# When the weights of the first MLP are narrowed, and when the right operands of the second token group are made

## The chip, the cores and the metric

The kernel runs on one core of a Trainium2 chip. The metric is the device time of one execution in microseconds (us). The engines are TensorE (PE; its weight loads are listed apart as PEld), VectorE (DVE), ScalarE (ACT) and GpSimd (POOL); SyncE (SP) issues almost all transfers.

## The reference, cut to what matters

```
kv  = einsum(k, v)                 # per batch and head, 64 x 64
out = einsum(q, kv);  out = out / rms(out) * g_norm
x   = out as [2304 tokens, 512]
x   = relu(x @ w_in)**2 @ w_out    # first MLP: 512 -> 2048 -> 512; its weights arrive as float64
for e in 0..3:                     # second MLP: 4 experts, 512 -> 1024 -> 512 each
    h    = relu(x @ w1[e])
    out += p[:, e] * (h @ w2[e])   # p: domain_probs, normalised
```

## The kernel before

**Precision.** Each float32 operand of a matmul is kept as two fp32r parts, a head (`hi`, made by ACT as a copy) and a remainder (`lo` = full - `hi`, made by a subtraction). A product is three matmuls for each slab of 128: `lo`·`hi`, `hi`·`lo`, `hi`·`hi`. `split` (L145) makes both parts: ACT, then POOL.

**Tiling.** The tokens form five blocks: 0 to 3 of 512 tokens, 4 of 256. The hidden width is cut into slices of 256. Slices 0 to 7 are the first MLP; slices 8 to 23 are the second MLP for the first token group (blocks 0, 1 and 4), slices 24 to 39 the same weights for the second group (blocks 2 and 3), loaded and prepared again (`slice_of`).

**Units.** The program is a list of small units, written out: `RAMP` (L49) for attention together with slices 0 and 1, `rest()` (L88) for all that follows. `run` (L542) calls one function per unit:

- `k`, `o`, `c`, `b`: attention and its normalisation.
- `f v.j.c` (`g1`): first product of slice v for block j, half c: 12 matmuls, then for the first MLP relu `r`, square `s`, head `hh` on ACT and remainder `hl` on POOL.
- `g v.j.c` (`g2a`): second product of the first MLP: 6 matmuls, then DVE adds to `acc` (L397).
- `s v.b.i` (`g1s`): the pair of blocks b and b+1 takes seven products in place of eight (`PRODUCTS`): the left operands are sums of weight tiles, the right operands are quarters of the pair's activations (`b11`, `b12`, `b21`, `b22`) and sums of them (`t1` to `t4`). 6 matmuls each, into the banks `pa` to `pd`; ACT copies the first result (`p1`), DVE forms `u2` (L480), `u4` (L482) and three more sums, each followed by relu (`hh`, L499) and remainder (`hl`, L500). `pc` and `pa`, `pd` are added to once more by later products, after `u4` and `p1` have been read.
- `h v.j.t` (`g2b`): second product of the second MLP: 6 matmuls, then DVE scales by p and adds (L522). The last slice of a group stores the rows.
- `x g.i` (`right`, L410): makes one tile of right operands for group g: two names of `OPS` at a time, for two slabs k each; `x0.4` makes the operand `xb` of block 4. The tiles `o` have the four buffers of the tag `xs`, which the first MLP's activations, and then group 1's operands, hold before. `t_sum` (L431) makes a sum anew for each name, with the sums that it is made of: 14 subtractions a group (L437). A sum's head is made by ACT (L428), its remainder by DVE (L429).
- `w` (`split_w`, L190): the next unit of weights, in a fixed order: four quarters for each of the slices 0 to 7, two halves for each later slice. Each begins the load of the unit two further on (`load_w(i + 2)`, SP queue, two raw buffers). A quarter of the first MLP is narrowed from float64 (`narrow`): six DVE steps (L171 to L185), a head on ACT (L221), two POOL steps (L222, L223). Half `.0` of a later slice (`operands`) is four sums on DVE (L238 to L241) and four splits into the left operands `a` and `a2`; half `.2` is two splits into `b`. The left operands have three buffers (`a2` two).

**What sets the order.** The units' place in the list is their priority. At build time a planner gives each engine its queue: it draws a ready instruction ahead where an engine would be idle, and gives out the buffers of a tag (the eight of `tmp` hold `r`, `s`, `u`, `k`, `p1`, `u2`, `u4`, the weight sums and the `t` sums) as the list asks for them. On the chip each engine runs its queue in order and waits where an input is late.

Each of the slices 2 to 7 is five blocks: `f` of a block, then `g` of the block before it, and here and there one `w`. A slice of group 1 is seven `s` with `h` of block 4 of the slice before among them, then `f` and `h` of the blocks. A slice of group 2 is seven `s`, each followed by an `h` of the slice before.

Of the kernel before, what the change touches and what calls it, by code (L numbers as in the profile page):

```python
# [10 lines left out]
F32 = mybir.dt.float32  # L11
# [4 lines left out]
ALU = mybir.AluOpType  # L16
PSUM = bass.MemoryType.PSUM

P = 128
# [11 lines left out]
NS1 = DFF // FS  # L31
NS2 = E * F2 // FS
# [20 lines left out]
b13 g0.1.1 c7 f0.2.1 g0.1.2 b15 b14 g0.1.3 w p g0.2.0 b17 g0.2.1 f0.3.0 f0.3.1 g0.2.2  # L53
g0.2.3 b16 w g0.3.0 g0.3.1 f1.0.0 g0.3.2 w f1.0.1 g0.3.3 f0.4.0 f0.4.1 g1.0.0 g1.0.1
g0.4.0 w g0.4.1 w g0.4.2 g1.0.2 w g0.4.3 g1.0.3 f1.1.0 f1.1.1 f1.2.0 f1.2.1 w w g1.1.0
g1.1.1 g1.1.2 g1.2.0 w w g1.2.1 g1.1.3 f1.3.0 g1.2.2 g1.2.3 w w f1.3.1 f1.4.0 g1.3.0
g1.3.1 g1.3.2 g1.3.3 w f1.4.1
""".split()


# [2 lines left out]
GRP2 = (((0, 1), (4,)), ((2, 3),))  # L63
# [7 lines left out]
def second(v, blk):  # L71
    if v < NS1:
        return [f"g{v}.{j}.{c}" for j in blk for c in range(KD)]
    return [f"h{v}.{j}.{t}" for j in blk[::-1] for t in range(BLK[j][1] // P)]


def merge(first, others):

    r, n = [], 0
    for i, u in enumerate(first):  # L80
        r.append(u)
        want = (i + 1) * len(others) // len(first)
        r += others[n:want]
        n = want
    return r


def rest():  # L88
    r, prev = [], (1, (NB - 1,))
    for v in range(2, NS1):  # L90
        for j in range(NB):
            r += [f"f{v}.{j}.{fc}" for fc in range(FC)] + second(*prev)
            if j < (4, 4, 4, 2, 2, 1)[v - 2]:
                r += ["w"]
            prev = (v, (j,))
            if v == NS1 - 1 and j >= 2:
                r += [f"x0.{j - 2}"]
    for g, group in enumerate(GRP2):
        for v in range(NS1 + g * NS2, NS1 + (g + 1) * NS2):
            for blk in group:  # L100
                b = blk[0]
                if v == NS1 and b == 0:
                    r += second(*prev) + ["x0.3"]
                    prev = (v, ())
                if v == NS1 and b == 4:
                    r += ["x0.4"]
                if v == NS1 + NS2:
                    r += [f"x1.{i}" for i in range(4)]
                if len(blk) == 2:
                    units = [f"s{v}.{b}.{i}" for i in range(7)]  # L110
                else:
                    units = [f"f{v}.{b}.{fc}" for fc in range(FC)]
                r += ["w"] * (blk == group[0]) + merge(units, second(*prev)) + ["w"] * (blk == group[-1])
                prev = (v, blk)
    return r + second(*prev)


@with_exitstack
def fused_kernel(ctx, tc, kvm, kvt, qt, g2, probs, w64, w32, out):
    nc = tc.nc  # L120
# [7 lines left out]
    tmp = ctx.enter_context(tc.tile_pool(name="tmp", bufs=8))  # L128
# [16 lines left out]
    def split(hi, lo, full):  # L145
        nc.scalar.activation(out=hi, in_=full, func=AF.Copy)  # L146
        nc.gpsimd.tensor_tensor(out=lo, in0=full, in1=hi.bitcast(F32), op=ALU.subtract)  # L147
# [60 lines left out]
    def split_first(i, v, c):  # L208
        if c == 0:
            w_t[v] = [  # L210
                wp.tile([P, 2, k, n], F32R, tag=t, name=f"{t}{v}")
                for t, k, n in (("a", KD, FS), ("b", FC, DM))
            ]
        w = w_t[v][c // 2]
        n = w.shape[2] // 2
        part = slice(c % 2 * n, c % 2 * n + n)
        r = raw.pop(i)
        hi, lo = (w[:, a, part, :].rearrange("p k f -> p (k f)") for a in range(2))
        if r.dtype == I64:
            top, rest = narrow(r, f"{v}_{c}")  # L220
            nc.scalar.activation(out=hi, in_=top, func=AF.Copy)  # L221
            nc.gpsimd.tensor_tensor(out=top, in0=top, in1=hi.bitcast(F32), op=ALU.subtract)  # L222
            nc.gpsimd.tensor_tensor(out=lo, in0=top, in1=rest, op=ALU.add)  # L223
        else:
            split(hi, lo, r)
# [178 lines left out]
    o_t, t_tmp = {}, {}  # L404

    def x_part(pair, name, k):

        return acc_t[pair[int(name[2]) - 1]][:, (int(name[1]) - 1) * 2 + k, :]

    def right(g, i):  # L410

        pair, *alone = GRP2[g]
        if i == 4:
            (j,) = alone[0]
            x_t[j] = xp.tile([P, 2, KD, BLK[j][1]], F32R, tag="xt", name=f"xb{j}", bufs=1)
            for k in range(0, KD, 2):
                split(*(x_t[j][:, a, k : k + 2, :] for a in range(2)), acc_t[j][:, k : k + 2, :])
            return
        o = xp.tile([P, 2, 4, 512], F32R, tag="xs", name=f"o{g}_{i}", bufs=4)
        for m, name in enumerate(OPS[i]):  # L420
            o_t[pair[0], name] = (o, m * 2)
            for k in range(2):
                hi, lo = o[:, 0, m * 2 + k, :], o[:, 1, m * 2 + k, :]
                if name[0] == "b":
                    split(hi, lo, x_part(pair, name, k))
                    continue
                full = t_sum(pair, name, k)
                nc.scalar.activation(out=hi, in_=full, func=AF.Copy)  # L428
                nc.vector.tensor_tensor(out=lo, in0=full, in1=hi.bitcast(F32), op=ALU.subtract)  # L429

    def t_sum(pair, name, k):  # L431

        b11, b12, b21, b22 = (x_part(pair, f"b{x}", k) for x in ("11", "12", "21", "22"))

        def sub(m, a, b):
            t = tmp.tile([P, 512], F32, tag="tmp", name=f"{m}_{name}_{pair[0]}_{k}")
            nc.vector.tensor_tensor(out=t, in0=a, in1=b, op=ALU.subtract)  # L437
            return t

        if name == "t3":  # L440
            return sub("t3", b22, b12)
        t1 = sub("t1", b12, b11)
        if name == "t1":
            return t1
        t2 = sub("t2", b22, t1)
        return t2 if name == "t2" else sub("t4", b21, t2)


    PRODUCTS = (
# [76 lines left out]
    def probs_p():  # L526
# [9 lines left out]

    unit = dict(
        k=att_kv, o=att_a, c=att_c, b=att_b, w=split_w, p=probs_p, f=g1, g=g2a, x=right, s=g1s, h=g2b
    )
    ext = None  # L540
# [32 lines left out]
    for name in rest():  # L573
        run(name)
# [47 lines left out]
```

## Time and profile before

| | |
|---|---|
| median of three timed runs | 1236.81 us (1235.37 to 1237.0) |
| the profiled execution | 1238.97 us, of which the profile's span 1237.2 us |
| PE, PEld busy | 1206.5 us (98%), 1012.0 us (82%) |
| DVE, ACT, POOL busy | 797.5 (64%), 427.3 (35%), 486.0 us (39%) |
| mean granted clock of PE | 0.991 of 2.4 GHz |

PE is busy almost throughout, and a busy PE can still be a slow one: its clock is granted at one of two levels, 1.2 or 2.4 GHz, and a matmul's busy time grows when it is low. So the time lost in a stretch is found by comparing its length with what its matmuls take at the rate of an undisturbed stretch. "<- DVE u L482" behind a wait names the instruction that ended it.

### The profile page before, as it was taken

How to read it: one execution, taken by the hardware profiler on the slowest of the kernel's cores; microseconds unless marked ns; L12 is line 12 of the kernel's file. 1: busy time of each engine (PE TensorE's matmuls, PEld its weight loads, DVE VectorE, ACT ScalarE, POOL GpSimd, SP SyncE). 2: the span in 40 equal slices, each digit the busy share in tenths (PEclk: the TensorE clock that was granted, in tenths of full speed). 3: DMA queues.
4: the chain of work that ended last, by engine and by line, in shares of the span. 5: the costliest groups of instructions: out<-in, count | busy, mean ns of one | idle time of the engine just before them, and what ended most of it. 6: DMA issues, size and time to landing. Idle time of an engine off the chain costs nothing.

```text
span 1237.2 us, 14956 instructions
## 1 busy us (share of the span) xinstructions
PE 1206.5 (98%) x5768; PEld 1012.0 (82%) x5768; DVE 797.5 (64%) x1229; ACT 427.3 (35%) x766; POOL 486.0 (39%) x382
## 2 busy tenths in 40 slices
PE   7999979999999999999999999999989999999998
PEld 6788768888888887888888888888868888888887
DVE  5977898657442249555665556655886666666655
ACT  3464334434434354222232222323423232323220
POOL 2557556544444246232222322233443333434310
PEclk9999989999999999999999999999989999999999
DMA  7711222111100000111101111111131111111101
GB/s 290 241 49 52 69 86 68 35 52 35 35 34 34 1 34 18 35 50 36 34 35 51 35 50 35 34 46 41 69 103 44 60 51 52 51 52 52 51 1 68
DMA packets 22247, 70.20 MB, mean 57 GB/s; under 512 B 2720, under 2 KB 2720, under 8 KB 22176
## 3 DMA queue, kind: packets, MB, share of 16 engines
q1 hardware_dynamic: 21888, 69.22, 16.2%
q8 instruction: 45, 0.74, 0.2%
q14 instruction: 26, 0.21, 0.1%
q10 hardware_dynamic: 288, 0.04, 0.0%
HBM read 64.52 MB, written 4.72 MB: 56 GB/s over the span
## 4 chain that ended last, share of the span: by engine, by line
PE 87%; DVE 10%; issue 1%; POOL 1%; DMA 1%; ACT 1%; DVEq 0%; ACTq 0%; POOLq 0%
PE p L512 31%; PE p L369 17%; PE p L390 12%; PE pc L467 7%; PE pd L467 7%; PE pa L467 7%; PE pb L467 3%; DVE t_t L437 2%; PE po L293 1%; PE pk L278 1%; DVE acc L397 1%; DVE o L429 1%; DVE k L185 1%; DVE u L175 1%; DVE k L179 1%
## 5 line engine op out<-in xcount | busy, mean ns | idle before, releaser
L512 PE MATMUL p<-b,hh 128*128 128x512 f32 x1152 | 382.7, 390 | 0.0
L522 DVE SCALAR_TENSOR_TENSOR acc<-p,p_sb,acc 128x512 f32<-128x512 f32 x270 | 202.2, 749 | 117.2 <-PE p L512 116.5
L512 PEld LDWEIGHTS p<-b,hh 128*128 128x128 f32 x1152 | 216.6, 188 | 44.5
L512 PE MATMUL p<-b,hl 128*128 128x512 f32 x576 | 224.5, 390 | 0.0
L369 PE MATMUL p<-x,a 128*128 128x512 f32 (+1 forms) x960 | 205.1, 369 | 0.0
L390 PE MATMUL p<-hh,b 128*128 128x512 f32 (+1 forms) x640 | 192.4, 374 | 3.0 <-ACT hh L146 2.9
L369 PEld LDWEIGHTS p<-x,a 128*128 128x128 f32 x960 | 168.1, 189 | 30.8 <-POOL x L147 0.2
L397 DVE TENSOR_TENSOR acc<-p,acc 128x512 f32<-128x512 f32 (+1 forms) x140 | 88.0, 633 | 128.3 <-PE p L390 127.4
L147 POOL TENSOR_TENSOR a<-raw,a 128x512 fp32r<-128x512 f32 x64 | 84.4, 1320 | 196.6 <-DVE pd L494 99.6
L147 POOL TENSOR_TENSOR hl<-s,hh 128x512 fp32r<-128x512 f32 (+1 forms) x80 | 100.7, 1262 | 145.8 <-ACT hh L146 125.4
L147 POOL TENSOR_TENSOR a<-w,a 128x512 fp32r<-128x512 f32 x64 | 86.1, 1345 | 175.9 <-ACT a L146 175.9
L390 PEld LDWEIGHTS p<-hh,b 128*128 128x128 f32 x640 | 118.2, 191 | 24.2 <-ACT hh L146 3.4
L390 PE MATMUL p<-hl,b 128*128 128x512 f32 (+1 forms) x320 | 120.3, 376 | 7.6 <-POOL hl L147 7.6
L512 PEld LDWEIGHTS p<-b,hl 128*128 128x128 f32 x576 | 108.4, 188 | 21.3
L147 POOL TENSOR_TENSOR b<-raw,b 128x512 fp32r<-128x512 f32 x64 | 82.3, 1306 | 77.5 <-ACT b L146 76.1
L467 PE MATMUL pc<-o,a 128*128 128x512 f32 x384 | 99.0, 393 | 4.4 <-DVE u L482 4.4
L467 PE MATMUL pd<-o,a 128*128 128x512 f32 x384 | 99.2, 393 | 0.9 <-DVE o L429 0.7
L467 PE MATMUL pa<-o,a 128*128 128x512 f32 x384 | 98.0, 390 | 1.8 <-ACT p L478 1.8
L374 ACT ACTIVATE r<-p 128x512 f32<-128x512 f32 (+1 forms) x80 | 44.1, 551 | 137.8 <-PE p L369 135.6
L467 PEld LDWEIGHTS pc<-o,a 128*128 128x128 f32 x384 | 72.7, 190 | 20.4 <-DVE u L482 5.3
L467 PEld LDWEIGHTS pd<-o,a 128*128 128x128 f32 x384 | 72.8, 190 | 16.9 <-DVE o L429 1.7
L467 PEld LDWEIGHTS pa<-o,a 128*128 128x128 f32 x384 | 72.1, 188 | 17.1 <-ACT p L478 2.2
(91 smaller groups left out, 1450.9 us busy)
## 6 DMA issues: line engine op xcount, KB each, us to landing
raw<-in_w SPq DMA_DIRECT2D x96, 512.0 KB, 3.7
kvm<-in_kvm SPq DMA_DIRECT2D x10, 512.0 KB, 3.6
q<-in_qt SPq DMA_DIRECT2D x18, 256.0 KB, 4.8
out<-acc SPq DMA_DIRECT2D x18, 256.0 KB, 2.1
kvs<-in_kvm SPq DMA_DIRECT2D x6, 512.0 KB, 7.3
kvt<-in_kvt SPq DMA_DIRECT2D x4, 256.0 KB, 5.9
p_raw<-in_probs ACTq DMA_DIRECT2D x1, 36.0 KB, 5.1
g_sb<-in_g ACTq DMA_DIRECT2D x1, 0.5 KB, 4.6
```

Source lines behind the costliest of these rows:

```text
L147: nc.gpsimd.tensor_tensor(out=lo, in0=full, in1=hi.bitcast(F32), op=ALU.subtract)
L175: nc.vector.scalar_tensor_tensor(out=u, in0=high, scalar=0xC0000000, in1=u, op0=ALU.bitwise_and, op1=ALU.bitwise_or)
L179: nc.vector.tensor_scalar(out=k, in0=high, scalar1=0x7FFFFFFF, scalar2=None, op0=ALU.bitwise_and)
L185: nc.vector.scalar_tensor_tensor(out=k.bitcast(F32), in0=low, scalar=2.0**-52, in1=k.bitcast(F32), op0=ALU.mult, op1=ALU.mult)
L369: nc.tensor.matmul(pt[:, :n], w, x, start=(i == 0), stop=(i == len(steps) - 1))
L374: nc.scalar.activation(out=r[:, :n], in_=pt[:, :n], func=AF.Relu)
L390: nc.tensor.matmul(pt[:, :n], w, h, start=(i == 0), stop=(i == len(steps) - 1))
L397: nc.vector.tensor_tensor(out=a, in0=pt[:, :n], in1=a, op=ALU.add)
L437: nc.vector.tensor_tensor(out=t, in0=a, in1=b, op=ALU.subtract)
L467: nc.tensor.matmul(pr[bank], x, y, start=(m == 0 and not more), stop=(m == len(steps) - 1), skip_group_check=more,)
L512: nc.tensor.matmul(pt, h, w, start=(i == 0), stop=(i == len(steps) - 1))
L522: nc.vector.scalar_tensor_tensor(out=a, in0=pt, scalar=pe, in1=a, op0=ALU.mult, op1=ALU.add)
```

## The change

In `RAMP` five `w` are dropped (between `g1.2.0` and `f1.4.1`). In `rest()` the slices 2 to 7 get 4, 4, 4, 4, 4, 2 units of weights (before: 4, 4, 4, 2, 2, 1), one behind each block's `g`. `x0.4` is made ahead of slice 8; slice 8 has no `w` of its own around its products and gets two behind each of its two parts; slice 23 has none, and the first slice of group 2 has two more behind it. So from slice 9 on, but for the stretch from slice 23 to the end of slice 24, the weights are one slice further ahead in the list. `x1.0` to `x1.3` stand among the products of slice 23, each behind the product that last reads the buffer it takes (before: behind that slice). `t_sum` keeps its sums, so a group makes 8 and not 14. The remainder of a sum's second slab is made by POOL.

```diff
@@ RAMP
-g1.1.1 g1.1.2 g1.2.0 w w g1.2.1 g1.1.3 f1.3.0 g1.2.2 g1.2.3 w w f1.3.1 f1.4.0 g1.3.0
-g1.3.1 g1.3.2 g1.3.3 w f1.4.1
+g1.1.1 g1.1.2 g1.2.0 g1.2.1 g1.1.3 f1.3.0 g1.2.2 g1.2.3 f1.3.1 f1.4.0 g1.3.0
+g1.3.1 g1.3.2 g1.3.3 f1.4.1
@@ rest()
-            if j < (4, 4, 4, 2, 2, 1)[v - 2]:
+            if j < (4, 4, 4, 4, 4, 2)[v - 2]:
                 r += ["w"]
...
+    r += second(*prev) + ["x0.3", "x0.4"]
+    prev = (NS1, ())
     for g, group in enumerate(GRP2):
         for v in range(NS1 + g * NS2, NS1 + (g + 1) * NS2):
+            turn = v == NS1 + (g + 1) * NS2 - 1 and g + 1 < len(GRP2)
             for blk in group:
                 b = blk[0]
-                if v == NS1 and b == 0:
-                    r += second(*prev) + ["x0.3"]
-                    prev = (v, ())
-                if v == NS1 and b == 4:
-                    r += ["x0.4"]
-                if v == NS1 + NS2:
-                    r += [f"x1.{i}" for i in range(4)]
                 if len(blk) == 2:
                     units = [f"s{v}.{b}.{i}" for i in range(7)]
+                    if turn:
+                        for at, i in ((7, 3), (6, 2), (4, 1), (2, 0)):
+                            units.insert(at, f"x{g + 1}.{i}")
                 else:
                     units = [f"f{v}.{b}.{fc}" for fc in range(FC)]
-                r += ["w"] * (blk == group[0]) + merge(units, second(*prev)) + ["w"] * (blk == group[-1])
+                w = [] if v == NS1 or turn else ["w"]
+                r += w * (blk == group[0]) + merge(units, second(*prev)) + w * (blk == group[-1])
                 prev = (v, blk)
+                if v == NS1 or (v - NS1) % NS2 == 0 and g:
+                    r += ["w"] * 2
@@ right()
                 full = t_sum(pair, name, k)
                 nc.scalar.activation(out=hi, in_=full, func=AF.Copy)
-                nc.vector.tensor_tensor(out=lo, in0=full, in1=hi.bitcast(F32), op=ALU.subtract)
+                engine = nc.gpsimd if k else nc.vector
+                engine.tensor_tensor(out=lo, in0=full, in1=hi.bitcast(F32), op=ALU.subtract)
@@ t_sum()
         def sub(m, a, b):
-            t = tmp.tile([P, 512], F32, tag="tmp", name=f"{m}_{name}_{pair[0]}_{k}")
-            nc.vector.tensor_tensor(out=t, in0=a, in1=b, op=ALU.subtract)
-            return t
-
-        if name == "t3":
-            return sub("t3", b22, b12)
-        t1 = sub("t1", b12, b11)
-        if name == "t1":
-            return t1
-        t2 = sub("t2", b22, t1)
-        return t2 if name == "t2" else sub("t4", b21, t2)
+            if (m, k) not in t_tmp:
+                t_tmp[m, k] = tmp.tile([P, 512], F32, tag="tmp", name=f"{m}_{pair[0]}_{k}")
+                nc.vector.tensor_tensor(out=t_tmp[m, k], in0=a(), in1=b(), op=ALU.subtract)
+            return t_tmp[m, k]
+
+        def t1():
+            return sub("t1", lambda: b12, lambda: b11)
+
+        def t2():
+            return sub("t2", lambda: b22, t1)
+
+        t = dict(
+            t1=t1, t2=t2, t3=lambda: sub("t3", lambda: b22, lambda: b12),
+            t4=lambda: sub("t4", lambda: b21, t2),
+        )[name]()
+        if name == "t4":
+            for m in ("t1", "t2", "t3", "t4"):
+                del t_tmp[m, k]
+        return t
```

## Rows read from the trace of the kernel before

**Rows 1.** The page: busy time by engine; PE busy tenths in 40 slices

```profile
PE 1206.5 (98%) x5768; PEld 1012.0 (82%) x5768; DVE 797.5 (64%) x1229; ACT 427.3 (35%) x766; POOL 486.0 (39%) x382
...
PE   7999979999999999999999999999989999999998
```

**Rows 2.** What PE waited for in the whole span

```profile
PE p L390 <- POOL hl L147: 7.6, 5, 2.6
...
PE pc L467 <- DVE u L482: 4.4, 2, 2.4
PE p L390 <- ACT hh L146: 2.9, 1, 2.9
...
PE pa L467 <- ACT p L478: 1.8, 1, 1.8
PE pd L467 <- DVE o L429: 0.7, 1, 0.7
```

**Rows 3.** Stretches: length; busy PE, PEld, DVE, ACT, POOL; clock; DMA share; rate

```profile
139.50:152.70 13.20, 10.40 (x38) 7.79 (x38) 10.25 (x12) 5.83 (x10) 9.90 (x8) 0.87 0.17 47
162.30:185.10 22.80, 15.80 (x63) 12.18 (x62) 22.53 (x28) 7.14 (x15) 14.34 (x11) 0.85 0.30 93
200.00:250.00 50.00, 50.00 (x245) 42.36 (x244) 34.93 (x49) 20.05 (x35) 24.36 (x20) 1.00 0.13 43
478.70:491.00 12.30, 9.88 (x45) 7.85 (x44) 11.75 (x20) 5.33 (x10) 7.25 (x5) 1.00 0.13 43
895.40:917.70 22.30, 17.67 (x62) 13.01 (x61) 18.80 (x28) 5.95 (x12) 7.43 (x6) 0.85 0.24 82
```

**Rows 4.** The chain that ended last, in order of time: start, duration

```profile
199.01 5.44 PE p L369 x24
...
491.12 1.43 PE p L369 x12
```

**Rows 5.** Timeline of ACT in the ramp: start, duration, instruction, idle before

```profile
170.65 0.63 ACT L221 ACTIVATE b<-u 128x512 fp32r<-128x512 f32 x1 [5.88 <-DVE u L180]
171.19 0.58 ACT L374 ACTIVATE r<-p 128x512 f32<-128x512 f32 x1
```

**Rows 6.** Groups by line and form: busy us, mean ns, idle before

```profile
L147 POOL TENSOR_TENSOR o<-acc,o 128x512 fp32r<-128x512 f32 x12 | 18.1, 1534 | 8.7 <-ACT o L146 8.7
...
L429 DVE TENSOR_TENSOR o<-t_t,o 128x512 fp32r<-128x512 f32 x16 | 15.9, 998 | 1.6 <-ACT o L428 1.6
L238 DVE TENSOR_TENSOR w<-raw 128x256 f32<-128x256 f32 x32 | 15.3, 478 | 0.0
...
L437 DVE TENSOR_TENSOR t_t<-acc,acc 128x512 f32<-128x512 f32 x12 | 11.8, 993 | 0.1
...
L437 DVE TENSOR_TENSOR t_t<-acc,t_t 128x512 f32<-128x512 f32 x12 | 9.6, 797 | 0.3
...
L437 DVE TENSOR_TENSOR t_t<-acc 128x512 f32<-128x512 f32 x4 | 5.6, 1398 | 0.0
```

**Rows 7.** Timeline of DVE in slice 23

```profile
873.65 0.69 DVE L482 TENSOR_TENSOR u<-pc,u 128x512 f32<-128x512 f32 x1 [0.65 <-PE pc L467]
...
877.29 1.77 DVE L437 TENSOR_TENSOR t_t<-acc,acc 128x512 f32<-128x512 f32 x1
...
882.05 0.68 DVE L500 SCALAR_TENSOR_TENSOR hl<-pc,hh 128x512 fp32r<-128x512 f32 x1
```

**Rows 8.** Timeline of PE in slice 23 and in slice 30 (group 2)

```profile
876.12 1.52 PE L467 MATMUL pc<-o,a 128*128 128x512 f32 x6
...
883.22 0.40 PE L512 MATMUL p<-b,hl 128*128 128x512 f32 x1
...
1029.20 1.52 PE L467 MATMUL pc<-o,a 128*128 128x512 f32 x6
```

**Rows 9.** Timeline of ACT at the start of slice 30

```profile
1021.34 0.63 ACT L146 ACTIVATE a<-raw 128x512 fp32r<-128x512 f32 x1 [0.86 <-DMA raw<-in_w]
```

**Rows 10.** The page's DMA issues: size, median us to landing

```profile
raw<-in_w SPq DMA_DIRECT2D x96, 512.0 KB, 3.7
```

## The prediction

> **What bounds the kernel now.** First I read the busy table and the span in 40 slices [rows 1]: TensorE (PE) is busy in 98% of the span, VectorE (DVE) in 64%, and PE's row of digits falls below 9 only in the first slice, in the sixth (about 155 to 186 us), in the thirtieth (about 897 to 928 us) and in the last. So the kernel is a PE stream, and an edit is worth what it does to PE's gaps. Next I read what PE waited for [rows 2]. Some 17 us of waits belong to the parts that the diff touches: 7.6 + 2.9 us on `hl` and `hh` (first MLP, ramp), and 4.4 + 1.8 + 0.7 us on `u`, `p` and `o` (where one set of right operands is left for the next).
>
> Waits understate the loss, because PE also runs slowly around them. So I compared, stretch by stretch, the time with the matmuls that it holds [rows 3]. The rate is that of undisturbed stretches: 24 matmuls of 512 columns in 5.44 us, 0.227 us each, and 12 of 256 columns in 1.43 us [rows 4].
>
> - 162.3 to 185.1 us (ramp: second half of `g1.3`, `f1.4.1`, `f2.0`): 48 wide matmuls and 12 narrow ones, 10.9 + 1.4 = 12.3 us of work in 22.8 us. Lost: 10.5 us. The granted clock is 0.85 on average here: after the waits it fell from 2.4 to 1.2 GHz for a while. DVE is busy for 22.5 of 22.8 us.
> - 478.7 to 491.0 us (the seven products of slice 8): 42 wide ones, 9.5 us of work, one wait of 2.4 us. Lost: 2.7 us with edges. The clock stays at 1.00.
> - 895.4 to 917.7 us (slice 24, first of group 2): 60 wide ones, 13.6 us in 22.3 us. Lost: 8.7 us, of which 4.5 us are waits [rows 2] (without the 2.4 us of slice 8); the rest is half clock, 0.85 granted on average.
> - 139.5 to 152.7 us: 36 wide ones, 8.2 us in 13.2 us. Lost: 5.0 us.
>
> What is late in the ramp is read from ScalarE's (ACT) queue [rows 5]. The first step of a narrowed quarter, L221, waits for DVE's chain (5.88 us the last time), and the relu `r` queued behind it starts only at 171.19 us, right after. PE then waits for that relu's `hh` and, behind GpSimd's (POOL) narrowing steps, for its `hl`.
>
> **The change part by part.**
>
> *Narrowing, slice by slice.* Five quarters (the last three of slice 3, the first two of slice 4) leave the end of the ramp; slices 2 to 7 get 22 `w` in place of 17. Each quarter takes its six DVE steps, one ACT and two POOL steps and the 512 KB load two units ahead (SP queue) along. Up to the first quarter of slice 3 the emitted order is the same, so the 5.0 us before 152.7 us stay. In the 10.5 us stretch every cause named in rows 5 goes. What can remain: `f1.3.1` ends only one narrow `f` (1.4 us) ahead of `g1.3`, and its relu, square, `hh` and `hl` must follow one another; the four `g1.3` are covered by their first halves (12 matmuls, 2.7 us) if these are queued first. I keep 1.0 us for it, under half of the longest waits of now (2.6 and 2.9 us): **9.5 us** gained, bounds 0 (the stall moves, see the rivals) and 10.5. What hides the moved work is the cover of a steady slice: from 200 to 250 us one quarter per block is narrowed, just as it will be to slice 6, and PE is busy for 50.00 of 50.00 us with DVE at 34.93 [rows 3]. Slice 3's quarters come before `f2.1` to `f2.3`, so they are ready ahead of `f3.0` and `g3.0`.
>
> *Sums kept, half of the remainders on POOL.* A group made 14 sums (28 in all, 27.0 us [rows 6], 0.96 each) and 8 remainders `lo` on DVE (1.00 each). It will make 8 sums and 4 remainders: DVE loses 6 x 0.96 + 4 x 1.00 = 9.8 us per group. POOL gets 4 remainders of a form that it has not in the trace; nearest are POOL's `o<-acc` at 1.53 us and the DVE step that it replaces at 1.00; I take 1.53, 6.1 us per group, beside its 7.3 busy us of the 12.3 us at slice 8 and 7.4 of the 22.3 us at slice 24 [rows 3]. In slice 8 it is the DVE backlog (11.75 busy of 12.3 us) that holds `u4`; 9.8 us less remove a 2.4 us wait. **2.5 us**, bounds 0 and 2.7. Moving `x0.4` ahead of slice 8 and two `w` behind it is costed at nothing: `xb` is first read by `f8.4`, after all seven products; without that cover it would cost one POOL pair, 3.1 us.
>
> The sums' means spread from 0.80 to 1.40 us by form [rows 6], and one sum of `x1` took 1.77 us [rows 7]. The Trainium skill, "SBUF — State Buffer", section "Who interferes with whom", says that a DVE instruction with two SBUF inputs and a GpSimd instruction that reads SBUF exclude each other for a whole instruction. By it, each of the four remainders moved to POOL may hold a sum up, and DVE would win only 9.8 - 6.1 = 3.7 us per group; that is still above the 2.4 us wait at slice 8, so the sum, 19.0 us by the rows, would be 18 to 19 by the rule. The 1.77 us agrees with such a hold.
>
> *Right operands of group 2 inside slice 23.* `x1.0` to `x1.3` are placed directly behind the product that last reads the buffer they take. The 22 steps on DVE (14 sums, 8 remainders) are now spread over slice 23 and the first products of slice 24; there `u4`, `p1` and a remainder came late. With 12 steps, begun earlier, I expect all to be done before slice 24 begins, and the 8.7 us go. But inside slice 23 the four sums of `x1.0` now stand ahead of `u4` (they share the `tmp` tag, and in the trace such steps run in emitted order). `u4` ended at 874.34 [rows 7] and the second `pc` product began at 876.12 [rows 8]: 1.8 us of room against 4 x 0.96 = 3.9 us, 2.1 us too late. Before `hl<-pc` (done 882.73 [rows 7], read by the `hl` matmul at 883.22 [rows 8]), the queue loses four `w` sums (4 x 0.48) and three `t` sums (3.1 us) and gets six sums and two remainders (7.8 us): 2.7 us more, 2.2 us too late. These are the same delay seen twice, or 4.3 us if not; below, 0, as PE has other products ready. I take 1.7: 8.7 - 1.7 = **7.0 us**, bounds 0.4 (4.3 us of waits and as much again for the clock, as in the stretch of now) and 8.7. The stores of group 1's rows keep their place in the SP queue relative to slice 23; no PE work waits for them.
>
> *Weights of the second MLP one slice earlier in the list.* In group 2 the four sums of slice v+2 now stand ahead of slice v's `u2` and `u4`. The raw tile is there at 1021.34 [rows 9]; sums (1.9), `u2`, `u4` (0.7 each, as in rows 7) end at 1024.6; the second `pc` product starts at 1029.20 [rows 8]. Room of 4.6 us: cost 0. In group 1 the raw tile lands a slice ahead: 0.
>
> Sum: 9.5 + 2.5 + 7.0 = **19.0 us**. The profiled execution took 1238.97 us (span 1237.2 and 1.8 around it), giving 1220; it lay 2.2 us above the median of the three timed runs, so for the median 1236.81 - 19.0 = **1217.8 us**, say 1218.
>
> **The rivals.**
> 1. *The narrowing stall moves.* The five quarters hold `hl` up in slices 2 to 6 as they did in the ramp. For it: the ramp lost 10.5 us over five quarters. Against: the 50 us at full PE. Gain 2.5 + 7.0 = 9.5, 1227 us. Chance 0.12.
> 2. *Slice 23 pays.* Both delays add up and the clock falls to half: part three gives 0.4, gain 12.4, 1224 us. For: DVE is the full engine there. Chance 0.15.
> 3. *Slower.* In group 2 the weight sums stand in the DVE queue ahead of `u2`; where raw lands over 4.6 us later than now, PE waits in each of some 15 slices. It decides at (19.0 + 2.5) / 15 = 1.4 us beyond that, 6 us late in all, when the median load takes 3.7 us from issue to landing [rows 10]. 1239.5 us or more. Against: nothing else loads then. Chance 0.04.
> 4. *Nothing.* Ready steps are already drawn ahead of their place now (sums of `x1` run from 877.29 on [rows 7], though listed behind slice 23), so the planner may give nearly the same queues. Against: the ramp's queues show the narrowing in listed order. 1236 us. Chance 0.03.
> 5. *More.* The loss before 152.7 us shrinks too: 1213 us. Chance 0.02.
>
> **How the numbers follow.** The forecast has the remaining 0.64; its own range is 1214 to 1222. Range with the rivals of the same sign: 1212 to 1228, which leaves out cases 3 and 4 and tails. A measurement of this kernel tells 0.2% (2.5 us) from no change: faster 0.93, same 0.03, slower 0.04.
>
> **What would show it.** After the change, no PE wait from 160 to 186 us and full clock there; one `w` group of steps per block to slice 6, PE full. Sums 16 in place of 28, remainders 8 on DVE and 8 on POOL; no `pc<-u` wait in slice 8; in the first slice of group 2 no wait and a clock of 1.00; perhaps 1 to 2 us in slice 23 at `pc` or at the first `h`. I am wrong if new `hl` or `b` waits stand in slices 2 to 6, if slice 23 loses over 4 us, or if `u` waits repeat slice by slice in group 2.

## The result, and the profile after

The changed kernel takes 1218.2 us (median of four runs, 1217.38 to 1221.71) where the kernel before takes 1236.9 in the same session. The ratio is 0.9857 with a 95% interval of 0.9836 to 0.9878, so it is faster by 1.2 to 1.6%. The prediction was 1218. A second session gave 1219.94 us and a ratio of 0.9864 (0.9845 to 0.9884).

The page after, which answers to [rows 1]: the busy times, PE's tenths in 40 slices, and the granted clock in tenths.

```profile
PE 1194.8 (98%) x5768; PEld 1004.0 (83%) x5768; DVE 801.6 (66%) x1209; ACT 424.3 (35%) x766; POOL 498.4 (41%) x390
...
PE   7999999999999999999999999999999999999998
...
PEclk9999999999999999999999999999999999999999
```

The holes in the sixth and the thirtieth slice are gone. What PE waited for, for [rows 2] (code lines have moved by 2 to 11: L390 is L392, L482 is L493, L499 is L510):

```profile
PE p L392 <- POOL hl L149: 4.1, 4, 1.5
PE pc L478 <- DVE u L493: 2.1, 1, 2.1
...
PE p L523 <- ACT hh L510: 0.5, 1, 0.5
```

Of `hl`, 7.6 us have become 4.1, and the 2.9 us on `hh` behind the narrowing are gone. The 4.4 us on `u` in slices 8 and 24 are gone too; the 2.1 us that are left on `u` are new, in slice 23, and so are the 0.5 us on `hh`. The stretches, for [rows 3] (columns as there): the one around the start of `f1.3.0` (148.63 us here), the ramp's second half, slice 8, slice 23, and slice 24.

```profile
139.50:152.70 13.20, 11.70 (x51) 9.49 (x51) 12.72 (x15) 4.53 (x8) 8.79 (x8) 1.00 0.13 41
152.70:175.00 22.30, 21.68 (x117) 18.35 (x116) 8.81 (x16) 8.72 (x17) 7.59 (x7) 1.00 0.08 25
465.00:477.00 12.00, 12.00 (x60) 9.98 (x60) 6.99 (x15) 4.45 (x8) 6.39 (x5) 1.00 0.13 44
853.20:882.50 29.30, 26.66 (x128) 22.02 (x127) 24.10 (x31) 12.47 (x23) 19.45 (x13) 1.00 0.18 58
882.50:897.40 14.90, 14.90 (x67) 12.37 (x66) 10.80 (x19) 7.20 (x14) 8.23 (x7) 1.00 0.47 162
```

PE is idle for 0.6 us in the ramp's second half, for nothing in slices 8 and 24, and for 2.6 us in slice 23. The clock is 1.00 in all five.

To see where time went in every kernel, I divided each trace at six starts of PE's timeline: the first matmul of `f1.3.0` and of `f2.1.0`, and the first `pb` matmul of slices 8 and 9 and of slices 23 and 25. "To f2.1.0" is the time from `f1.3.0` on; "slice 8" is the time from the `pb` of slice 8 to that of slice 9, and "turn" the time from the `pb` of slice 23 to that of slice 25, so slices 23 and 24 together. Undisturbed, the turn would take 39.6 us: 26.04, which a slice of group 1 takes from slice 9 on, and 13.60, the shortest time seen from the `pb` of slice 24 to that of slice 25.

| profiled kernel | start of f1.3.0 | to f2.1.0 | slice 8 | turn | span |
|---|---|---|---|---|---|
| before | 152.68 | 35.26 | 26.04 | 48.36 | 1237.2 |
| before_again | 148.40 | 35.76 | 27.65 | 47.04 | 1233.7 |
| pace_only | 150.02 | 25.98 | 27.66 | 47.02 | 1225.5 |
| sums_only | 148.48 | 35.80 | 23.32 | 45.60 | 1227.8 |
| place_only | 152.32 | 35.19 | 26.04 | 49.68 | 1238.1 |
| after | 148.63 | 25.95 | 23.57 | 42.86 | 1215.6 |
| after_again | 150.43 | 25.97 | 23.53 | 43.65 | 1218.1 |
| x10_late | 152.63 | 25.97 | 23.69 | 44.76 | 1221.6 |
| lo_dve | 152.33 | 25.96 | 23.90 | 48.12 | 1224.9 |
| x1_later | 151.80 | 25.97 | 23.51 | 40.55 | 1216.4 |
| both | 146.26 | 26.01 | 23.54 | 41.01 | 1211.4 |
| both_2 | 147.76 | 26.01 | 23.53 | 41.11 | 1213.0 |

From before to after the spans differ by 21.6 us: 4.05 ahead of `f1.3.0`, 9.31 in the ramp's second half, 2.47 at slice 8, 5.50 at the turn, and 0.27 between `f2.1.0` and slice 8. From slice 9 to 23 and from slice 25 to PE's last matmul the two agree to 0.01 us.

### The profile page after: what moved, and what is told of

Its sections match the earlier page's. It is cut to its first block, busy times and chain, and to the rows that moved or that the text cites. A ratio compares the mean times of both kernels' runs of the same rounds, so it can differ in the third digit from the quotient of the medians.

```text
span 1215.6 us, 14933 instructions
## 1 busy us (share of the span) xinstructions
PE 1194.8 (98%) x5768; PEld 1004.0 (83%) x5768; DVE 801.6 (66%) x1209; ACT 424.3 (35%) x766; POOL 498.4 (41%) x390
## 4 chain that ended last, share of the span: by engine, by line
PE 91%; DVE 5%; DMA 1%; issue 1%; POOL 1%; ACT 1%; SPq 0%; POOLq 0%; DVEq 0%; ACTq 0%
PE p L523 32%; PE p L371 18%; PE p L392 14%; PE pa L478 7%; PE pd L478 7%; PE pc L478 7%; PE pb L478 4%; PE po L295 1%; DVE u L177 1%; PE pk L280 1%; DMA kvs<-in_kvm 1%; DMA raw<-in_w 1%; DVE k L187 1%; DVE u L173 1%; DVE k L181 0%
## 5 line engine op out<-in xcount | busy, mean ns | idle before, releaser
L533 DVE SCALAR_TENSOR_TENSOR acc<-p,p_sb,acc 128x512 f32<-128x512 f32 x270 | 199.7, 746 | 49.3 <-PE p L523 48.5
L392 PE MATMUL p<-hh,b 128*128 128x512 f32 (+1 forms) x640 | 189.9, 370 | 0.1
L149 POOL TENSOR_TENSOR hl<-s,hh 128x512 fp32r<-128x512 f32 (+1 forms) x80 | 100.9, 1264 | 118.9 <-ACT hh L148 114.7
L392 PEld LDWEIGHTS p<-hh,b 128*128 128x128 f32 x640 | 116.5, 188 | 20.8 <-POOL b L225 0.5
L523 PEld LDWEIGHTS p<-b,hl 128*128 128x128 f32 x576 | 108.2, 188 | 21.6 <-DVE hl L511 0.3
L392 PE MATMUL p<-hl,b 128*128 128x512 f32 (+1 forms) x320 | 118.3, 370 | 4.1 <-POOL hl L149 4.1
L148 ACT ACTIVATE a<-raw 128x512 fp32r<-128x512 f32 x64 | 40.1, 628 | 142.3 <-DMA raw<-in_w 110.7
```

The costliest lines, as they stand in the source:

```text
L392: nc.tensor.matmul(pt[:, :n], w, h, start=(i == 0), stop=(i == len(steps) - 1))
L523: nc.tensor.matmul(pt, h, w, start=(i == 0), stop=(i == len(steps) - 1))
L533: nc.vector.scalar_tensor_tensor(out=a, in0=pt, scalar=pe, in1=a, op0=ALU.mult, op1=ALU.add)
```

## The experiments

**The kernel before, once more** (no edit).

> The kernel before, once more, for the spread of what no edit touches. My theory (4.0 of the 21.6 us by which the two profiled executions differ lie in code that the change leaves alone: 2.45 us to the end of the attention's first wait on hl at 121 us, 1.6 us from there to the start of f1.3.0; they are the execution's, the clock's after a wait above all): in this execution at least one of the two stretches comes out over 1 us shorter than in the profile of before (121.1 and 31.6 us). Rival (the change's): both stretches repeat within 0.3 us.

One run, 1235.48 us. The first wait on `hl` ends at 118.39 us in place of 121.08, and `f1.3.0` follows 30.0 us later in place of 31.6. Both stretches came out shorter, by as much as in the changed kernel, so the 4.05 us ahead of `f1.3.0` are the execution's and not the change's. Against this trace the changed kernel wins 9.81 + 0.27 + 4.08 + 4.18 - 0.23 = 18.1 us.

Slice 8 went the other way. In the kernel before, PE waited 2.42 us for `u4` there, and its clock stayed at 1.00 [rows 3]. Here the wait is the same, but the clock falls right behind it; six matmuls take 2.45 us in place of 1.65. The PE timeline and the stretches of before_again:

```profile
482.96 2.45 PE L467 MATMUL pc<-o,a 128*128 128x512 f32 x6 [2.42 <-DVE u L482]
```

```profile
139.50:152.70 13.20, 11.71 (x51) 9.68 (x52) 12.95 (x15) 3.22 (x6) 8.78 (x8) 1.00 0.13 40
474.90:487.20 12.30, 9.88 (x38) 7.66 (x37) 11.76 (x20) 5.12 (x9) 7.23 (x5) 0.86 0.13 43
```

So the same wait cost 2.4 us in one execution and 4.0 in another. Ahead of `f1.3.0` it is the reverse: behind the same waits of 1.3 and 1.5 us the clock was 0.87 before [rows 3] and is 1.00 here. The same work stands 2.7 to 4.3 us earlier in this trace, from 136.8 to 148.4 us; the clock is 1.00 there too.

**The narrowing alone.**

```diff
-g1.1.1 g1.1.2 g1.2.0 w w g1.2.1 g1.1.3 f1.3.0 g1.2.2 g1.2.3 w w f1.3.1 f1.4.0 g1.3.0
-g1.3.1 g1.3.2 g1.3.3 w f1.4.1
+g1.1.1 g1.1.2 g1.2.0 g1.2.1 g1.1.3 f1.3.0 g1.2.2 g1.2.3 f1.3.1 f1.4.0 g1.3.0
+g1.3.1 g1.3.2 g1.3.3 f1.4.1
...
-            if j < (4, 4, 4, 2, 2, 1)[v - 2]:
+            if j < (4, 4, 4, 4, 4, 2)[v - 2]:
```

> The kernel before with one part of the change alone: the five quarters narrowed at the end of the ramp go to slices 2 to 7; sums, remainders and the place of the right operands stay as before. My theory (the ramp's loss is the queueing of the five quarters on ACT, DVE and POOL, and a steady slice has room for them): from the start of f1.3.0 to the start of f2.1.0 some 26 us in place of 35.3, the 2.4 us wait of slice 8 on u and the 8.7 us lost in slice 24 stay as they were; 9 to 10 us less in all, 1226 to 1228 us where the kernel before takes 1237. Rival (the stall only moves): new waits on hl in slices 2 to 6 add up to several us, 1232 to 1237. Second rival (the narrowing also eases the stretch before 152 us): that stretch takes 1.6 us or more less than before, 1224 or less.

1227.44 us, ratio 0.9934 (0.9918 to 0.9951) to 1235.59. From `f1.3.0` to `f2.1.0` it takes 25.98 us; slice 8 and the turn are those of before_again. The waits and the stretch:

```profile
PE pc L467 <- DVE u L482: 4.4, 2, 2.4
PE p L390 <- POOL hl L147: 4.1, 4, 1.5
```

```profile
152.70:176.00 23.30, 22.68 (x122) 19.11 (x122) 8.27 (x16) 9.78 (x18) 7.00 (x7) 1.00 0.08 24
```

No `hl` wait is left behind 175 us, and from there to slice 8 it takes 292.14 us, as before. Nothing moved into slices 2 to 6: the first rival falls. The ramp gained 9.3 to 9.8 us, by the trace of before that it is held against, and the median shows 8.15; in the profiled execution `f1.3.0` started 1.6 us later than in before_again.

**The kept sums and POOL's remainders alone.**

```diff
-                nc.vector.tensor_tensor(out=lo, in0=full, in1=hi.bitcast(F32), op=ALU.subtract)
+                engine = nc.gpsimd if k else nc.vector
+                engine.tensor_tensor(out=lo, in0=full, in1=hi.bitcast(F32), op=ALU.subtract)
...
+            if (m, k) not in t_tmp:
+                t_tmp[m, k] = tmp.tile([P, 512], F32, tag="tmp", name=f"{m}_{pair[0]}_{k}")
```

> The kernel before with another part alone: sums kept and half of the remainders on POOL; the narrowing and the place of the right operands in the list stay as before. My theory (slice 8 is held by DVE's backlog; the loss in slice 24 is a matter of DVE's backlog and of the place both): slice 8 takes 23.6 us in place of 26.1, slice 24 wins a part, 3 to 6 of its 8.7 us, slice 23 loses nothing; 5.5 to 8.5 us less in all, 1228.5 to 1231.5 us where the kernel before takes 1237. Rival (fewer DVE steps alone are enough at slice 24): it wins 8 us or more without the 3.2 us that the changed kernel loses in slice 23, 1226 or less. Second rival (place alone matters there): slice 24 wins under 1 us, 1234.

1229.71 us, ratio 0.9952 (0.9937 to 0.9967): 5.9 us less. Slice 8 takes 23.32 us, as expected, and has no wait. The turn gains only 1.4 us against before_again (2.8 against before), less than the 3 to 6 that I gave it. Slice 24 still waits, 1.8 us for `u` and 1.6 in two shorter waits. That the time fell into the range all the same is slice 8's doing: against before_again, with its half clock, it gave 4.3 us where I had 2.5. The wait on `u`:

```profile
PE pc L476 <- DVE u L491: 1.8, 1, 1.8
```

**The place inside slice 23 alone.**

```diff
                     units = [f"s{v}.{b}.{i}" for i in range(7)]
+                    if v == NS1 + NS2 - 1:
+                        for at, i in ((7, 3), (6, 2), (4, 1), (2, 0)):
+                            units.insert(at, f"x1.{i}")
...
-                if v == NS1 + NS2:
-                    r += [f"x1.{i}" for i in range(4)]
```

> The kernel before with a third part alone: the right operands x1.0 to x1.3 stand inside slice 23, as in the change, but their sums are made anew (14 in the group) and all remainders stay on DVE. My theory (the place pays only because the kept sums and the remainders on POOL make DVE's share of it small enough; DVE has some 8 us more to do in slice 23 than in the changed kernel): from the pb product of slice 23 to that of slice 25 it takes 46 us or more, where the kernel before takes 47.0 to 48.4 and the changed kernel 42.9, with waits of over 4 us in slice 23; in all 1233 to 1237 us, the kernel before 1236. Rival (the place alone is what gives the 5 us): 43 to 44 us there, 1231 to 1232 in all. Second rival (worse than before): over 48.4 us there.

1238.7 us, ratio 1.002 (1.0011 to 1.0029): slower than before by 0.1 to 0.3%. The second rival holds, with its bound of 48.4 us passed: the turn takes 49.68. The theory has its waits of over 4 us in slice 23, but the time lies above its 1233 to 1237. Slice 24 has no wait, so the place does what it says, but slice 23 pays 10 us for it. PE's waits, two in slice 23 (2.1 of the 4.5 us on `u`, the rest is slice 8's), and DVE's timeline from `u2` to the step `pc` on which relu and `hh` of the next half depend:

```profile
PE p L513 <- ACT hh L500: 5.8, 1, 5.8
...
PE pc L468 <- DVE u L483: 4.5, 2, 2.4
```

```profile
871.88 0.69 DVE L481 TENSOR_TENSOR u<-pb,p 128x512 f32<-128x512 f32 x1 [2.04 <-PE pb L468]
...
882.82 3.48 DVE L438 TENSOR_TENSOR t_t<-acc 128x512 f32<-128x512 f32 x2
886.23 0.74 DVE L523 SCALAR_TENSOR_TENSOR acc<-p,p_sb,acc 128x512 f32<-128x512 f32 x1
886.89 2.77 DVE L430 TENSOR_TENSOR o<-t_t,o 128x512 fp32r<-128x512 f32 x2
889.58 0.69 DVE L490 TENSOR_TENSOR pc<-pc,u 128x512 f32<-128x512 f32 x1
```

`pc` is added 17.7 us after `u2`; ahead of it stand sums and remainders for group 2, which nobody reads before slice 24. The weights are not what differs from the changed kernel there: in this run, too, their first sum comes behind all of it, at 906.60 us.

**`x1.0` one place later.**

```diff
-                        for at, i in ((7, 3), (6, 2), (4, 1), (2, 0)):
+                        for at, i in ((7, 3), (6, 2), (4, 1), (3, 0)):
```

> The changed kernel with one unit moved by one place: the right operands x1.0 stand behind the third product of slice 23 in place of the second, so the four sums that they make stand behind u4 in DVE's list. My theory (the 2.1 us wait on u4 in slice 23 is those four sums ahead of it): the wait on u4 goes, the time from the start of slice 23 to the first product of slice 24 falls from 29.3 to some 26.5 us, and slice 24 stays at 12.2 us: 2 to 3 us less than the changed kernel, 1215 to 1216.5. Rival (DVE has too much to do in slice 23 in any order): the wait moves to the pc or hh that comes after, slice 23 stays over 28.5 us, the time is that of the changed kernel, 1218. Second rival (x1.0 is now late itself): a wait in the first products of slice 24 of 2 us or more.

1221.49 us, ratio 0.9882 (0.9865 to 0.9899). The changed kernel's interval overlaps; the turn, 44.76 us where the changed kernel has 42.86 and 43.65, says that it is no better. The profiled execution is the slowest of four, with a mean clock of 0.996; the two at 0.999 took 1220.1 and 1220.2 us. PE's timeline has no wait on `u4` now, but a longer one on `hh`; DVE's shows why:

```profile
874.67 2.07 PE L523 MATMUL p<-b,hh 128*128 128x512 f32 x4 [3.48 <-ACT hh L510]
```

```profile
860.38 0.69 DVE L491 TENSOR_TENSOR u<-pb,p 128x512 f32<-128x512 f32 x1 [2.07 <-PE pb L478]
861.64 0.69 DVE L493 TENSOR_TENSOR u<-pc,u 128x512 f32<-128x512 f32 x1 [0.57 <-PE pc L478]
...
873.30 0.69 DVE L500 TENSOR_TENSOR pc<-pc,u 128x512 f32<-128x512 f32 x1
```

The four sums were what `u4` waited for, as my theory said. The gain of 2 to 3 us did not come, as the rival said: the sums now stand ahead of `pc`, 12.9 us after `u2`.

**All remainders back on DVE.**

```diff
-                engine = nc.gpsimd if k else nc.vector
-                engine.tensor_tensor(out=lo, in0=full, in1=hi.bitcast(F32), op=ALU.subtract)
+                nc.vector.tensor_tensor(out=lo, in0=full, in1=hi.bitcast(F32), op=ALU.subtract)
```

> The changed kernel with all remainders of the sums back on DVE (four more DVE steps and four fewer POOL steps in each group). My theory (DVE is the full engine in slice 23, and each of its steps counts): the four steps of 0.7 to 1.0 us lengthen the stretch from the pb product of slice 23 to that of slice 25 by 2 to 3.5 us, from 42.9 to 45 to 46.4, and slice 8 stays without a wait on u, as 5.8 us fewer on DVE are enough for a wait of 2.4; 1220 to 1222 us, the changed kernel 1218. Rival (a remainder on POOL holds a DVE step up for as long as it saves; seen in sums of 1.7 us beside POOL steps): the stretch stays within 0.7 us of 42.9. Second rival: slice 8 has its wait of 2 us again.

1226.53 us (1220.99 to 1228.7), ratio 0.991 (0.9878 to 0.9942). Slice 8 has no wait on `u` (one of 0.3 us on `hl`): six sums less are enough there. The turn takes 5.3 us more, above the 2 to 3.5 that I gave. Only 1.9 of them are waits (4.5 us in slice 23, where the changed kernel has 2.6). Most of the rest goes with two falls of the clock, 0.90 granted from 858.6 to 893.1 us, where slice 23 of the changed kernel had 1.00 in its first trace. One of the four runs, 1220.99 us at a mean clock of 0.997, lies in the range that I gave; the other three have 0.991 to 0.993. The added waits are hardly the load: DVE's remainders grow from 9.4 to 14.5 us for both groups, while its `t` sums shrink from 20.1 to 16.9, so it has 1 us more to do in a group. The rows speak for the order. Ahead of `pc` stand six remainders in place of three, and the last two take 3.28 us, behind 1.11 us of waiting for ACT:

```profile
872.95 3.28 DVE L431 TENSOR_TENSOR o<-t,o 128x512 fp32r<-128x512 f32 x2 [1.11 <-ACT o L430]
876.15 0.69 DVE L499 TENSOR_TENSOR pc<-pc,u 128x512 f32<-128x512 f32 x1
```

**The right operands spread over slice 23.**

```diff
-                        for at, i in ((7, 3), (6, 2), (4, 1), (2, 0)):
+                        for at, i in ((7, 1), (5, 0)):
                             units.insert(at, f"x{g + 1}.{i}")
                 else:
                     units = [f"f{v}.{b}.{fc}" for fc in range(FC)]
+                    if turn:
+                        units = [units[0], f"x{g + 1}.2", units[1], f"x{g + 1}.3"]
```

> The changed kernel with the four right operands of group 2 spread over slice 23 more evenly: x1.0 behind the fifth product, x1.1 behind the seventh, x1.2 and x1.3 behind the two first halves of block 4. My theory (the waits on u4, 2.1 us, and on hh, 0.5 us, and the 3.5 us on hh of the run with x1.0 one place later, are the products' own DVE steps standing behind steps for group 2 that nobody needs before the end of the slice): both waits go, the stretch from the pb product of slice 23 to that of slice 25 takes 39.6 to 40.2 us in place of 42.9; some 3 us less than the changed kernel, 1215. Rival (slice 23 has more DVE work than it can hold in any order): waits of 2 us or more appear at the first products of slice 24 or on a PSUM tile that acc has not read yet, the stretch takes over 42 us.

1215.43 us, ratio 0.9834 (0.9817 to 0.985). Slice 23 loses nothing (26.04 us): the same steps on the same engines, with `pc` at 864.74 us, 5.4 after `u2`. The turn takes 40.55 us, 2.3 less than in the changed kernel and 0.35 above the range that I gave; 0.9 are lost at the first products of slice 24, where DVE's last remainder of `x1.3` is late and `u4` behind it. The timelines of DVE and of ACT:

```profile
884.15 1.37 DVE L434 TENSOR_TENSOR o<-t,o 128x512 fp32r<-128x512 f32 x1 [3.34 <-ACT o L432]
```

```profile
882.96 0.63 ACT L150 ACTIVATE a<-raw 128x512 fp32r<-128x512 f32 x1 [9.10 <-DMA raw<-in_w]
883.50 0.62 ACT L432 ACTIVATE o<-t 128x512 fp32r<-128x512 f32 x1
```

DVE waits for a head that ACT could have made at 879 us (its sum ended at 877.79 + 1.32); in ACT's queue a split of the next weights stands ahead of it and waits for its load.

**Spread, and three quarters of the ramp later.** The edit above, and this one beside it:

```diff
-g0.4.0 w g0.4.1 w g0.4.2 g1.0.2 w g0.4.3 g1.0.3 f1.1.0 f1.1.1 f1.2.0 f1.2.1 w w g1.1.0
-g1.1.1 g1.1.2 g1.2.0 g1.2.1 g1.1.3 f1.3.0 g1.2.2 g1.2.3 f1.3.1 f1.4.0 g1.3.0
+g0.4.0 w g0.4.1 w g0.4.2 g1.0.2 g0.4.3 g1.0.3 f1.1.0 f1.1.1 f1.2.0 f1.2.1 g1.1.0
+g1.1.1 g1.1.2 w g1.2.0 g1.2.1 g1.1.3 f1.3.0 w g1.2.2 g1.2.3 f1.3.1 f1.4.0 w g1.3.0
```

> The run with the right operands spread, and in the ramp three narrowed quarters moved behind the second halves that wait for hl: one from ahead of g0.4.3 to behind g1.1.2, two from ahead of g1.1.0 to behind f1.3.0 and f1.4.0. My theory (the two waits of 1.26 and 1.50 us on hl between 138 and 142 us, in every kernel so far, are the same queueing of relu and hl behind narrowing steps as in the part of the ramp that the change cleared): both go, and with them the half clock that follows them in some executions; f1.3.0 starts 2.5 to 4 us earlier, in all 5 to 7 us less than the changed kernel, 1211 to 1213. Rival (the moved quarters hold up the halves behind them): as much waiting on hl between 142 and 175 us, 1215 like the run with the right operands spread.

1211.81 us, ratio 0.9802 (0.9788 to 0.9817): below both intervals of the changed kernel. The two waits are gone (the two that are left on `hl` end at 119.6 and 158.0 us), and PE is never idle from 128 to 147 us, at full clock. The waits on `hl` of the whole span, and the stretches:

```profile
PE p L394 <- POOL hl L151: 1.4, 2, 0.7
```

```profile
128.00:141.00 13.00, 13.00 (x59) 10.78 (x58) 9.71 (x14) 7.99 (x14) 7.21 (x6) 1.00 0.23 76
141.00:147.00 6.00, 6.00 (x28) 4.95 (x28) 5.18 (x7) 0.62 (x1) 3.69 (x3) 1.00 0.22 58
```

From the first matmul of `f1.1.0` to that of `f1.3.0` it takes 19.0 us, where x1_later takes 22.4 and after_again 24.0; nothing came back later (26.01 us to `f2.1.0`).

**The changed kernel again, and `x1.2` and `x1.3` one place earlier.** The first has no edit.

```diff
-                        units = [units[0], f"x{g + 1}.2", units[1], f"x{g + 1}.3"]
+                        units = [f"x{g + 1}.2", units[0], f"x{g + 1}.3", units[1]]
```

> The changed kernel once more, for the spread of what no edit touches and as the neighbour of the next run. My theory (of the 21.6 us between the two profiled executions about 4 lie in unchanged code and are the execution's): the changed stretches repeat within 0.3 us where PE waits are not followed by half clock (26.0 us from f1.3.0 to f2.1.0, 23.6 in slice 8, 42.9 from the pb product of slice 23 to that of slice 25), while f1.3.0 starts anywhere from 148.4 to 152.7; 1217 to 1222 us. Rival: all of it repeats, f1.3.0 within 0.3 us of 148.6.

> The run with both edits, with x1.2 and x1.3 one place earlier each (ahead of the two first halves of block 4 in place of behind them). My theory (the 0.6 to 0.7 us wait on u in slice 24 is x1.3's remainder, late at 885 us on DVE, and the acc steps behind it): that wait goes, the stretch from the pb product of slice 23 to that of slice 25 takes 39.6 to 40.2 us in place of 41.0; 1 us less than the run with both edits, 1211. Rival (the earlier steps delay the hh of the last product again): a wait on hh in slice 23, 41 us or more.

The changed kernel: `f1.3.0` starts 1.8 us later than the first time, and the clock falls behind the same waits behind which it stayed up there: behind 1.51 us on `hl` at 141.46 us, and behind 2.12 us on `u` in slice 23 (six matmuls in 2.68 us, where they took 1.66).

```profile
864.76 2.68 PE L478 MATMUL pc<-o,a 128*128 128x512 f32 x6 [2.12 <-DVE u L493]
```

The ramp and slice 8 repeat within 0.05 us; the turn does not (43.65), since its wait was followed by half clock, the condition that the expectation named.

The other run: 1212.47 us, ratio 0.9806 (0.979 to 0.9821), the same as without the edit. My theory of the last 0.9 us fell: the turn takes 41.11 us, and the waits are still there. The steps were asked for earlier and came at the same point, behind the load:

```profile
879.53 0.63 ACT L150 ACTIVATE a<-raw 128x512 fp32r<-128x512 f32 x1 [7.63 <-DMA raw<-in_w]
880.07 1.14 ACT L432 ACTIVATE o<-t 128x512 fp32r<-128x512 f32 x2
```

```profile
880.72 1.37 DVE L434 TENSOR_TENSOR o<-t,o 128x512 fp32r<-128x512 f32 x1 [2.59 <-ACT o L432]
```

## Why the prediction was right

**The narrowing, 9.5 us predicted.** Measured 9.31 and, against the second trace of before, 9.81; alone 9.3 and 9.8 in the same stretch. One wait of 0.62 us on `hl` is left at 160.37 us, where I kept 1.0. The cover named for the moved steps held: from `f2.1.0` to slice 8 no kernel lost anything. Two readings ahead of it were loose. The stretch from 162.3 us holds all 24 matmuls of `g1.3`, as its count of 48 says, not their second half. And of the 17 us of waits that I gave to the diff, 3.5 on `hl` stand ahead of 152.7 us, where it changes nothing; they are most of the 4.1 that are left.

**Sums and remainders at slice 8, 2.5 us.** 2.47 against the one trace of before, 4.08 against the other, in which the clock fell behind the wait. The mechanism, DVE's backlog ahead of `u4`, is shown by sums_only, and lo_dve shows that the kept sums alone are enough for it. The working had a term wrong: DVE was to lose 9.8 us a group. By line and form, for [rows 6]:

```profile
L241 DVE TENSOR_TENSOR w<-w,raw 128x256 f32<-128x256 f32 x32 | 27.4, 857 | 0.0
...
L441 DVE TENSOR_TENSOR t<-acc,t 128x512 f32<-128x512 f32 x8 | 9.4, 1178 | 0.2
L432 DVE TENSOR_TENSOR o<-t,o 128x512 fp32r<-128x512 f32 x8 | 9.4, 1174 | 1.1 <-ACT o L430 1.0
L441 DVE TENSOR_TENSOR t<-acc,acc 128x512 f32<-128x512 f32 x4 | 5.4, 1348 | 0.1
L441 DVE TENSOR_TENSOR t<-acc 128x512 f32<-128x512 f32 x4 | 5.3, 1358 | 0.0
```

The 16 sums take 20.1 us (28 took 27.0), the eight remainders 9.4 (16 took 15.9): 13.4 us less for both groups, 6.7 a group. The steps that stay have become longer, the sums 1.26 us each in place of 0.96. POOL's added steps account for a part: in lo_dve, which has eight of them fewer, the same 16 sums take 16.9 us, 1.06 each. Slice 23 shows how, on DVE and POOL:

```profile
856.84 0.68 DVE L441 TENSOR_TENSOR t<-acc,acc 128x512 f32<-128x512 f32 x1
857.56 1.67 DVE L441 TENSOR_TENSOR t<-acc,t 128x512 f32<-128x512 f32 x1
859.15 1.78 DVE L441 TENSOR_TENSOR t<-acc,acc 128x512 f32<-128x512 f32 x1
...
862.24 0.69 DVE L493 TENSOR_TENSOR u<-pc,u 128x512 f32<-128x512 f32 x1
...
868.10 0.68 DVE L500 TENSOR_TENSOR pc<-pc,u 128x512 f32<-128x512 f32 x1
```

```profile
856.85 3.53 POOL L149 TENSOR_TENSOR o<-acc,o 128x512 fp32r<-128x512 f32 x2 [2.63 <-ACT o L148]
861.67 3.49 POOL L432 TENSOR_TENSOR o<-t,o 128x512 fp32r<-128x512 f32 x2 [1.29 <-ACT o L430]
```

The first sum starts just ahead of POOL's first step and takes 0.68 us. POOL's first two steps end at some 858.6 and at 860.38 us, and each of the next two sums, 1.67 and 1.78 us long, ends 0.6 us behind one of them, as if it had stood still until POOL was done. `u4`, which reads one operand from PSUM, runs in 0.69 us beside POOL's next step. The Trainium skill, "SBUF — State Buffer", section "Who interferes with whom", says that a DVE instruction with two SBUF inputs contends with a GpSimd instruction that reads SBUF; these rows agree, with 1.67 and 1.78 us in place of 0.68. By that rule alone I had 3.7 us a group; the measured 6.7 lies between it and 9.8.

**The turn, 7.0 us.** Measured 5.50, and 4.18 against the second trace. This is the step that was mis-sized, in its cost: "I take 1.7" was 3.2 us in one trace and 4.0 in the other, at the 4 us that the prediction itself had named as a sign of being wrong. The 1.7 lay below its own working, 2.1 to 2.2 us, on the ground that PE has other products ready; they covered nothing. The first part was right to the decimal: `u4` was named as 2.1 us too late, for the four sums of `x1.0` ahead of it, and PE waited 2.12 us. The second part, "the same delay seen twice", was nearly right too: only 0.51 us more, on `hh`. What I left out is that PE loses more around a wait than the wait (0.6 us in the one trace, half clock in the other), though I had used just that in reading the kernel before and in the lower bound. The gain of 8.7 us at slice 24 came in full against the first trace and is 7.4 against the second: there too the clock decides.

What the runs add is that the two parts of the change need each other. Alone, the kept sums give 1.4 to 2.8 us at the turn, and the place loses 1.3 to 2.6; together they give 4.2 to 5.5 (in a kernel that also moves the weights, which no run does alone). The measure is the time on DVE from `u2` to `pc` in slice 23, against PE's waits there:

| | before | sums_only | x1_later | after | x10_late | lo_dve | place_only |
|---|---|---|---|---|---|---|---|
| `u2` to `pc`, us | 7.9 | 8.0 | 5.4 | 11.9 | 12.9 | 15.9 | 17.7 |
| PE's waits, us | 0 | 0 | 0 | 2.6 | 3.5 | 4.5 | 7.9 |

Up to 8 us PE waits for nothing; from 11.9 on its waits are more than half of what lies above 8, and nothing between was measured. It isn't how much DVE has to do, but what stands in its queue ahead of the step that PE needs next: x1_later has all the steps of the changed kernel and no wait in slice 23.

**What cost next to nothing.** `x0.4` ahead of slice 8, and the weights a slice earlier: no wait from slice 24 on, and from slice 25 to the start of PE's last matmul 313.93 us in both kernels. They were never run alone; slice 8 takes 0.2 us more than in sums_only, which has neither. The weight sums themselves became longer (857 ns for the form of L241, 457 before, 721 in after_again), unseen by PE. None of rivals 1, 3 and 4 came; of rival 2, the loss in slice 23, a part; and what looks like rival 5, the stretch before 152.7 us, is the execution's, as before_again and after_again show.

**The sum.** The changed parts gave 17.6 us against one trace of before and 18.3 against the other, for 19.0; the medians differ by 18.7 and, in the second session, 16.7. That the forecast met the first median to 0.2 us is in part luck of the executions; it would hold to 2 us in either session.

## What to carry to other kernels

Steps that prepare the next phase belong behind those that the running phase waits for, not merely behind the last reader of the buffer they take: read on the full engine what stands between two steps that the critical engine needs. Two edits that each look small or worse may need each other, so a part that loses alone is not to be dropped before it was tried with the other. And where the clock may fall behind a wait, a removed wait is worth its length or, here, 0.8 to 2.8 us more, by the execution; compare stretch by stretch, and the same kernel twice, before a microsecond is put down to an edit.

## What the runs showed of the hardware

PE's clock did not answer to the length of a wait alone. Behind the same 2.42 us in slice 8 it stayed at 2.4 GHz in one execution of the kernel before and fell to 1.2 GHz in another (so too in place_only and pace_only); behind the same 1.5 us on `hl`, the last wait ahead of `f1.3.0`, it fell in before and after_again and stayed up in before_again and after. A fall cost 1.6 us at either place (27.65 for 26.04, and 31.6 for 30.0 from the first wait on `hl` to `f1.3.0`), but 2.8 at the second in lo_dve (32.8), and 0.8 in slice 23 of the changed kernel (30.05 for 29.26). What decides between executions was not tried and stays open; taking the wait away settles it, as in the run with both edits.

The start of the kernel varies as well. In the four traces of the kernel before and of the changed one, which have the same units in the same order up to there, the first wait on `hl` ended at 118.4, 118.6, 118.9 and 121.1 us. From 10 to 20 us PE began 65 matmuls in before_again and 49 in before, while the transfers moved 403 and 402 GB/s. The cause was not looked for.
